# An FFT convolution block: times split 64 by 16 with two groups of times on the partitions, smaller tiles in the first and last step, a new order

## The chip, the cores and the metric

The kernel runs on one core of one Trainium2 chip. The metric is the device time in microseconds (us). Five engines work side by side, each through its own queue in order: PE (matmuls, with PEld loading weights), DVE, ACT, POOL (named G in the order below) and SP, which here only issues transfers. Transfers run on 16 DMA engines.

## The reference

```python
def _A_ref(q, k, v, shift_k, ssm_k, ssm_D):            # 2048 times, 512 channels
    k_shift = sum(k_pad[:, t:t + S, :] * shift_k[:, ks - 1 - t] for t in range(4))
    kv = k_shift * v
    y = irfft(rfft(kv, padded to 2S) * rfft(ssm_k, padded to 2S))[:, :S]   # long convolution
    y = y + kv * ssm_D
    return q * y
...
x = A_q
h = x + _A_ref(_layernorm(x), A_k, A_v, A_shift_k, A_ssm_k, A_ssm_D)
h2 = h + _B_ref(_layernorm(h), B_w1, B_w2, B_w3, B_w4)
```

`_B_ref` is a block with four matmuls: layer norm, w1 (512 x 512), GELU, a shift in time by -1, +1, -2 and +2 of four groups of channels, w2, a residual, then layer norm, w3 (512 x 1792), GELU, w4 and a residual. All inputs and the output are bfloat16.

## The kernel before

The 2048 times are cut into two halves s of 1024. Time t = 1024 s + 8 p + b lies on partition p, in block b (0 to 7); so a row of `q`, `v` and the output is 8 consecutive times of one half. The long convolution is done by halves, with odd-frequency transforms of length 2048 of each half of the filter (F0, F1) and of kv (A0, A1). The first half of y is A0 x F0, the second A0 x F1 + A1 x F0. The transform of 1024 times is split 32 by 32, p = 4 n + l.

The steps, with the short names that are used here; a name is followed by its half or signal and numbers (S1:F0.3.0):

- Lf, Lk, Lv, Lq: loads of the filter, of k (already transposed, with the taps of the short filter behind each row), of v and q. K (L432) is the short convolution as matmuls against diagonals of the taps (dg, L295); KV (L446) multiplies it by v on DVE.
- S1 (step1, L382): first step, 128-row matmuls onto 32 columns; the table f1 is zero where a row belongs to another l. E1 copies PSUM to bfloat16. X (L405): eight transfers of 256 KB per signal, SBUF to SBUF, that exchange partition and block. S2 (step2, L408): second step, on 64x32 tiles. E2 copies out, or for F1 combines with F0.
- P (L474): products of spectra on DVE; I2 (L484): first inverse step, on 32x64 tiles; EV copies out; XI (L495): 16 transfers of 256 KB in all that bring the result back into the order of times; I1 (inv1, L498): last inverse step, full 128x128 matmuls, two accumulated.
- H (L615): q (y + ...) by DVE, with Y the normalised q (its row statistics are Q, L505, then QV, QP, QN). HS, uw, rr, hn: layer norms. hb, lb: normalised rows; LT/TE and LX/EX transpose them, by PE (flip) or by DMA (turn). W, U: w1 and GELU; X2: w2; S, R: sums; M, G: w3 and GELU; O: w4; Z: the last sum; OUT: store.

What runs in which order is written out by hand as a string, ORDER: each word has the number of a task, its engine (P, V for DVE, A, G for POOL, S for SP) and its PSUM slots. Tasks are added with their dependencies in `body`; a program emits them in ORDER's order, so each engine's queue stands in the order of its words, and an instruction that waits holds all that stands behind it on its engine. The figures in braces in the `add` calls are a planner's costs and set nothing at run time. The buffer r_z holds the first-step results of A1 and also receives XI, so S1 of A1 waits for I1 of the first half (the zdeps of forward1, L395).

SP's queue begins with the loads of the first half; Q:0.0 to Q:0.7 stand on DVE behind the KV of the first half.

Of the kernel before, what the change touches and what calls it, by code (L numbers as in the profile page):

```python
# [17 lines left out]
KW = NB * 129 + 8  # L18
# [13 lines left out]
004S 029P0 000S 002S 003S 005S 008S 031V 037V 001S 030P 063P23 006S 055P45 009S 057P67 064V 007S 056A 038G 065P01 010S 058A 019S 059P45 033V 045G  # L32
061P23 060A 087P60 039G 036V 062A 095P71 046V 042V 066A 093P4 032G 043V 047A 074S 101P5 044A 034G 015S 094V 051P23 022S 088V 053P01 035G 023S 052A
040V 072S 089P4 024S 054A 049G 091P6 021S 090V 073S 041A 097P2 096V 050G 070S 092V 099P3 048A 069S 102V 068S 107P01 098V 109P67 017S 100V 108A 103P45
067S 110V 111P23 018S 104A 115P01 071S 113P67 112A 323V 105P45 324V 116A 211P20 106V 114A 117P01 212V 119S 118A 084P4567 326V 085A 081P2301 123S 329V
086V 120S 083A 215P4 020S 082A 330V 124S 078P0167 327V 125S 217P5 080A 216V 121S 079A 075P2367 012S 218V 011S 325V 076A 127P4501 016S 319V 328V 122S
077A 219P21 129V 126S 331G 128A 013S 220V 130P6701 139V01 132A 141V23 131A 133P4501 332G 134A 140P23670 147V45 142P 135A 333G 149V67 143A 337G0
148P45011 155V01 150P 343G1 144A 145S 221P2 340G2 157V23 152A 146S 334G3 014S 151A 136P6701 222V 137V 138A 156P23452 153S 158P 154S 163V45 225P0 159A
223P1 160A 165V67 161S 164P67230 162S 226V 166P 224V 175P45 167A 168V 213P0 176A 169S 183P67 214V 170S 185P23 184A 187P45 315S 186V 177P01 188A 189P67
178V 179P23 190A 181P45 180V 171P67 028S 182A 172P01 338V 192S 231P45 196S 335V 339A 349G0 173P23 316S 344V 336A 346G3 193S 341V 235P67 232A 355G1  # L40
195S 347V 174P10 236A 352G2 191S 350V 237P45 198S 358G 342A 356V 202P6723 197S 348A 353V 194S 345A 359G 204V 239P01 238A 371G 203V 241P23 240A 227P45
242A 229P01 372G 360V 228V 230A 199P6723 247S 361G0 373V 233P45 351A 364G1 200V 362P00 234A 374G2 365P1 384V 366A 377G3 208P6745 245S 363V 354A 375P11
243S 201V 385G 367P0 376A 244S 357A 378P1 386V 246S 369P2 379A 390V0 318S 209V 397G 387A1 382P3 248S 370A 250S 388P12 210V 368A 398G 391P6 249S 380P7
383A 389A 027S 392V 399G 251P2345 263V01 381A 393P0 253A 026S 400G3 265V23 395P1 025S 252A 317S 403V2 205P6745 396A 267V45 401P23 394A 404P3 502P1
402A 206V 405A 506P0 503V 408P2 507V 504A 406P3 269V67 508A 409A 264P67011 558V 407A 266P 207V 268P 559G 270P 560G 498P2 271A 272V 561G1 510P3 564G0
499V 274S 494P4 501V 273S 562P50 511V 565P6 514P7 563A 495V 566A 411V 254P0123 496A 567P50 515V 256A 275V01 569P4 568A 577P6 277V23 570A 257P2345 578A
412V 573P7 259A 255V 571P6 258A 279V45 579P4 572A 574A 281V67 575P5 580A 516A 276P01232 414V 500A 278P 513V 280P 576A 615G 512V 282P 581P6 505V 283A
616G 517V 284A 617G 413V 621G3 287V01 618A2 619P71 587G 622P4 582V 260P0123 620V 583S 584P5 623V 588G 262A 289V23 589G 291V45 591A1 590G0 293V67
624P40 593S 261V 636P6 592S 625A 634P7 416V 509V 288P23010 635A 594S2 290P 299V01 292P 285S 294P 301V23 628P4 296A 632P7 303V45 629A 298S 637A 626P0
286S 633A 305V67 630P1 295A 410V 627A 297S 300P67231 417V 631A 302P 415V 304P 306P 418V 641P4 307A 419G 308A 309S 310S 420V 421V0 427G3 638P0 424G1  # L50
430V2 585V 642V 497V 311P16 639V 312P72 640S 422V 643S 313P35 425V 423A 433G0 428V 314P40 426A 431V 439A3 595P10 445G 442V1 432A 603P2 436V2 429A 437V
597P6 596A 434V 446G 605P7 598A 438A 447V 599P1 448V2 435A 451G3 322V 458V 607P5 600A 470V 459G 449P33 452P6 601P1 450V 453A 471G 460V 604A 440V 454P6
602A 472G 441V 461A2 456P3 443V 474G1 462A3 444V 473G0 608A 476S 606A 612P2 482V 475S 457A 463S 483G 464S 609P1 484V 477S0 485A1 486G0 455A 487S 321V
488S 465S1 518P0 522P3 489S2 480P4 523V 478P5 519V 524A 468P3 520A 481A 466P7 644V 521V 645G 490P6 467A 525V 646G 469A 492P0 610V 320G 479A 647V2
534P3 491A 648V3 649S 493A 650S 542P4 535V 554P5 537V 536A 538P3 651S3 555V 546P7 543V 556A 586S 545V 526P1 544A 611S 539V 530P6 547V 540A 550P3 527V
672G 652P00 529V 531V 658P1 673G 528V 656P5 659A 674V 532V 653A 675G1 662P4 657A 549V 676G0 660P7 551V 678S 654P5 552V 661A 677S 664P3 553V 655A 756G
548A 533V 663A 679S0 700V 665A 666P6 701G 702V 703V3 704G2 613V 669P7 757G 667V 706S 705S 541V 758G 557V 759G0 728G 680P10 729G 686P0 681A 730V 731V1
682P5 732G2 670V 687A 688P4 684P3 707S1 760G3 689A 692P2 668S 761S 693A 733S 685A 734S 708P60 714P4 735S2 712P1 720P0 671S 713A 762S 710P2 721A 715A
716P3 711A 736P10 683A 763S3 717A 742P0 709A 614S 737A 748P6 743A 738P4 749A 764P50 772P7 776P6 774P2 777A 765A 766P3 775A 768P6 767A 773A 744P5 769A
740P1 770P0 741A 739A 771A 778P2 718P4 779V 780S 719A 725P3 722P4 726V 727S 781P7 723V 724S 690P4 782V 783S 691A 697P6 745A 694P7 746P1 695V 698V 696S  # L60
747A 750P0 699S 753P2 751V 752S 754V 755S
# [32 lines left out]
def body(ctx, tc, fx, kt, q, v, sd, w1, w2, w3, w4, out):  # L94
# [18 lines left out]
    HX = 130  # L113
# [8 lines left out]
    r_h = raw("r_h", DC * NB * HX)  # L122
# [7 lines left out]
    kT = [[kw[:, s, c, 0:NB * 129].rearrange("p (b x) -> p b x", b=NB) for c in range(DC)] for s in range(2)]  # L130
    kvs = r_kv[:].rearrange("p (g b d) -> p g b d", g=2, b=4)

    def z1v(r):
        return view(r, 0, G, "p (b h d) -> p b h d", b=4, h=4)
# [10 lines left out]
    wv = view(r_z, 0, G, "p (k h d) -> p k h d", k=NB, h=2)  # L145
# [3 lines left out]
    h1T = [view(r, 0, DC * NB * HX, "p (c b x) -> p c b x", c=DC, b=NB) for r in (r_h, r_f0)]  # L149
# [6 lines left out]
    GHOME = ((r_v, NB * D), (r_kv, 0), (r_v, NB * D), (r_kv, 0), (r_f0, DC * NB * HX), (r_a0, 0), (r_a0, GS), (r_f1, 0))  # L156
    gbs = [view(r, lo, GS, "p (f x) -> p f x", f=FC) for r, lo in GHOME]
    nbx = ct("nbx", 2, D)
    nbt = [r_k[:, DC * F:DC * F + D], r_k[:, DC * F + D:DC * F + 2 * D], nbx[:, 0, :], nbx[:, 1, :]]
# [8 lines left out]
    f1 = ct("f1", 8, 2, 2, 2, 4)  # L168
    f2 = ct("f2", 2, 32, 4)
# [41 lines left out]
    u1a, u1b = early(64), [early(64)]  # L211
    pool.iota(u1a.rearrange("p (t h c k) -> p t h c k", t=2, h=4, c=2), pattern=[[2048, 2], [128, 4], [0, 2], [512, 4]], base=32, channel_multiplier=0)
    pool.iota(u1b[0].rearrange("p (a c k) -> p a c k", a=8, c=2), pattern=[[0, 8], [1024, 2], [0, 4]], base=3072, channel_multiplier=0)
    l4 = small("l4", 4)
    pool.iota(l4[:], pattern=[[1, 4]], base=0, channel_multiplier=0)
    pn = small("pn", 2)
    vec.tensor_scalar(out=pn[:, 0:1], in0=pi[:], scalar1=2, scalar2=None, op0=SHR)
    vec.tensor_scalar(out=pn[:, 1:2], in0=pi[:], scalar1=3, scalar2=None, op0=AND)
    nf = small("nf", 2, F32)
    vec.tensor_copy(nf[:], pn[:])  # L220
    s1 = early(64, BF16)
    mk = small("mk", 4, F32)

    vec.scalar_tensor_tensor(out=u1b[0], in0=u1a, scalar=nf[:, 0:1], in1=u1b[0], op0=MUL, op1=ADD)
    vec.tensor_scalar(out=u1b[0], in0=u1b[0], scalar1=4095, scalar2=None, op0=AND)
    act.activation(s1, u1b[0], ACT.Sin, bias=negpi[:], scale=SC)
    vec.tensor_scalar(out=mk[:], in0=l4[:], scalar1=nf[:, 1:2], scalar2=None, op0=OP.is_equal)
    for i in range(2):
        for j in range(2):
            vec.tensor_scalar(out=f1[:, :, i, :, j, :], in0=s1.rearrange("p (a c k) -> p a c k", a=8, c=2),  # L230
                              scalar1=mk[:, 2 * i + j:2 * i + j + 1], scalar2=None, op0=MUL)
    make_identity(nc, ident[:])
    wf = early(72, F32).rearrange("p (o b) -> p o b", o=9)
    pool.memset(wf[:, 0:8, :], 0.0)
    for o, terms in enumerate((((4, 16), (2, 8), (0, 4), (1, 2), (5, 1)), ((6, 64), (7, 1)), ((3, -1024), (7, 3072)), ((3, 3072),),
                               ((5, 4), (6, 8), (0, 128), (1, 256), (2, 512), (3, 1024), (4, 2048)), ((6, 64), (0, 16), (1, 32), (2, 8), (7, 1)),
                               ((3, -3072), (7, 3072)), ((5, 2), (4, 1)))):
        for b, w in terms:
            pool.memset(wf[:, o, b:b + 1], float(w))
# [192 lines left out]
    def shift(g, c):  # L432
        s, b4 = divmod(g, 2)

        def f(e, sl):
            o = ps[:, sl[0], :]
            for i, d in enumerate((0, 1, 2, 3, -1, -2, -3)):
                j0, j1 = max(0, -d), min(3, 3 - d)
                bb, x = 4 * b4 + d, 1
                if bb < 0:  # L440
                    bb, x = bb + NB, 0
# [402 lines left out]
```

## Time and profile before

| what | value |
|---|---|
| runs | 214.49, 215.71, 216.97 us; median 215.71 |
| the profiled execution | 213.26 us, of which the span is 211.6 |
| granted TensorE clock | 1.000 |
| PE / DVE / ACT busy, 0 to 60 us | 51.3 / 55.5 / 50.4 us |
| PE / DVE / ACT busy, 60 to 114 us | 51.8 / 50.1 / 35.9 us |
| PE / DVE / ACT busy, 114 to 212 us | 92.6 / 39.2 / 39.3 us |
| DMA share and rate in these three stages | 0.84 and 286 GB/s; 0.58 and 174; 0.27 and 64 |
| first products (P) begin | 30.4 us |
| I1 of the first half begins, of the second half | 48.5 us, 113.9 us |

The page gives busy times per engine over the span and in 40 equal slices (a digit is tenths of a slice), the chain of waits followed back from the last instruction, and the costliest groups of instructions. A group's line has the line of the kernel, the engine, the operation, its output and input tiles with sizes, the count, the busy time and the mean duration. The answers by stage list, for each stretch, the busy time of each engine with the number of instructions in brackets, then the granted clock, the mean share of the 16 DMA engines and the rate. Transfers are listed with their size and the time from issue to landing:

```profile
r_z<-r_vs SPq DMA_DIRECT2D x16, 256.0 KB, 3.9
r_k<-in_kt_dram SPq DMA_DIRECT2D x8, 260.0 KB, 4.6
r_v<-in_v_dram SPq DMA_DIRECT2D x4, 512.0 KB, 7.3
r_f<-r_f SPq DMA_DIRECT2D x8, 256.0 KB, 5.2
r_q<-in_q_dram SPq DMA_DIRECT2D x8, 256.0 KB, 5.7
...
out_dram<-r_v SPq DMA_DIRECT2D x16, 128.0 KB, 1.9
```

r_z<-r_vs is XI; r_f<-r_f is X of F0; out_dram is OUT.

### The profile page before, as it was taken

The numbers are of one execution on the slowest core, as the hardware profiler recorded it, in microseconds if no ns is written. First come the engines' busy times: TensorE is split into PE (matmuls) and PEld (weight loads), VectorE is DVE, ScalarE is ACT, GpSimd is POOL, SyncE is SP. The second block draws the span as 40 slices with busy tenths as digits, with TensorE's granted clock in tenths as the row PEclk, the third lists the DMA queues.
The fourth block names the chain that finished last, engine by engine and source line by source line (L and its number), as shares of the span: only waits on it lengthen the run. The fifth ranks groups of instructions, "written<-read, shape, count | busy, mean of one in ns | idle before, by whom it ended". The sixth has DMA issues, their size and how long they took to land.

```text
span 211.6 us, 5040 instructions
## 1 busy us (share of the span) xinstructions
PE 195.7 (93%) x1964; PEld 116.2 (55%) x1980; DVE 144.8 (68%) x302; ACT 125.5 (59%) x206; POOL 80.1 (38%) x177
## 2 busy tenths in 40 slices
PE   6899769898889999979999999989999999999992
PEld 5454323442248546636744884645848888645450
DVE  6998999999999999999868971559972000112031
ACT  3979989787999658943751883364623565301010
POOL 7850059804888140287044683212765000000000
PEclk9999999999999999999999999999999999999999
DMA  6999895976948995000693008533146440010011
GB/s 173 313 403 397 321 325 222 256 205 237 371 169 294 332 435 147 0 28 13 89 232 92 27 22 181 98 69 82 42 107 154 102 74 0 3 50 34 16 50 50
DMA packets 30809, 32.86 MB, mean 155 GB/s; under 512 B 20545, under 2 KB 22594, under 8 KB 30530
## 3 DMA queue, kind: packets, MB, share of 16 engines
q1 hardware_dynamic: 30786, 32.55, 50.8%
q8 instruction: 15, 0.25, 0.5%
q14 instruction: 8, 0.07, 0.1%
HBM read 13.14 MB, written 4.46 MB: 83 GB/s over the span
## 4 chain that ended last, share of the span: by engine, by line
PE 59%; DVE 13%; ACT 12%; DMA 6%; issue 3%; POOL 3%; SPq 3%; DVEq 0%; ACTq 0%; POOLq 0%
PE ps L777 21%; PE ps L790 18%; ACT r_a L257 5%; PE ps L722 5%; PE ps L699 5%; PE ps L484 3%; DVE r_v L616 3%; DMA r_dg<-dhb 2%; DMA r_a<-r_a 2%; PE ps L502 2%; PE ps L413 2%; DMA r_k<-in_kt_dram 2%; DVE r_f L425 2%; DVE r_dg L307 1%; DVE r_p L474 1%
## 5 line engine op out<-in xcount | busy, mean ns | idle before, releaser
L777 PEld LDWEIGHTS <-r_k 128*128 128x128 bf16 x448 | 43.5, 98 | 7.7 <-issue 1.2
L792 DVE TENSOR_TENSOR r_v<-ps,r_v 128x512 bf16<-128x512 f32 x16 | 10.7, 686 | 42.4 <-PE ps L790 42.4
L474 DVE TENSOR_TENSOR r_p<-r_a,r_f 128x2048 bf16<-128x2048 bf16 x24 | 28.7, 1240 | 1.0 <-PE ps L484 0.6
L777 PE MATMUL ps<-r_dg,r_k 128*128 128x256 bf16 x224 | 25.6, 273 | 0.1
L257 ACT CAST r_a<-ps 128x1024 bf16<-128x1024 f32 x23 | 22.2, 1026 | 3.0 <-PE ps L413 2.8
L781 ACT ACTIVATE r_f<-ps 128x512 bf16<-128x512 f32 x14 | 7.8, 599 | 20.6 <-PE ps L777 20.6
L613 POOL TENSOR_SCALAR z_t<-r_q,qrs,qnm 128x512 f32<-128x512 bf16 x11 | 13.0, 1188 | 12.6 <-DVE r_v L616 12.0
L442 PE MATMUL ps<-r_dg,r_k 128*128 128x256 bf16 (+3 forms) x108 | 15.2, 284 | 1.6 <-ACT r_f L257 0.8
L257 ACT CAST r_vs<-ps 128x1024 bf16<-128x1024 f32 x14 | 13.7, 1032 | 4.9 <-PE ps L484 4.9
L725 DVE SCALAR_TENSOR_TENSOR r_q<-r_v,hrr,ps 128x512 bf16<-128x512 bf16 x16 | 11.4, 742 | 5.9 <-PE ps L722 3.7
L781 ACT ACTIVATE r_a<-ps 128x512 bf16<-128x512 f32 x14 | 7.8, 606 | 12.2 <-PE ps L777 12.2
L257 ACT CAST r_f<-ps 128x1024 bf16<-128x1024 f32 x14 | 13.2, 1023 | 3.0 <-PE ps L389 2.8
L442 PEld LDWEIGHTS <-r_k 128*128 128x128 bf16 x112 | 9.5, 98 | 9.5 <-issue 4.8
L484 PE MATMUL ps<-r_p,ttab 32*64 32x512 bf16 x384 | 13.3, 379 | 1.0 <-DVE r_p L474 0.8
L699 PEld LDWEIGHTS <-r_fx 128*128 128x128 bf16 x128 | 12.3, 98 | 3.2 <-DMA r_dg<-dhb 0.6
L600 ACT ACTIVATE junk<-r_v 128x512 bf16<-128x512 bf16 x14 | 8.9, 635 | 7.3 <-DVE r_v L616 7.1
L777 PE MATMUL ps<-xtx,r_k 128*128 128x256 bf16 x112 | 13.0, 273 | 0.0
L600 ACT ACTIVATE junk<-r_q 128x512 bf16<-128x512 bf16 x12 | 7.6, 630 | 9.2 <-DVE r_q L725 9.1
L777 PE MATMUL ps<-xty,r_k 128*128 128x256 bf16 x112 | 12.7, 272 | 0.0
L790 PE MATMUL ps<-w4s,r_f 128*128 128x512 bf16 x54 | 12.5, 379 | 0.1
L748 POOL TENSOR_TENSOR xrr<-xrr,mhalf 128x2 f32<-128x2 f32 x8 | 7.2, 900 | 14.2 <-DVE xrr L745 13.8
L389 PEld LDWEIGHTS <-f 128*32 128x32 bf16 x256 | 6.1, 95 | 11.3 <-issue 7.5
(183 smaller groups left out, 374.7 us busy)
## 6 DMA issues: line engine op xcount, KB each, us to landing
r_z<-r_vs SPq DMA_DIRECT2D x16, 256.0 KB, 3.9
r_k<-in_kt_dram SPq DMA_DIRECT2D x8, 260.0 KB, 4.6
r_v<-in_v_dram SPq DMA_DIRECT2D x4, 512.0 KB, 7.3
r_f<-r_f SPq DMA_DIRECT2D x8, 256.0 KB, 5.2
r_q<-in_q_dram SPq DMA_DIRECT2D x8, 256.0 KB, 5.7
r_a<-r_a SPq DMA_DIRECT2D x8, 256.0 KB, 4.2
r_f<-r_a SPq DMA_DIRECT2D x8, 256.0 KB, 4.2
r_a<-r_z SPq DMA_DIRECT2D x8, 256.0 KB, 4.1
```

The lines of the kernel that those rows point to most:

```text
L257: (act.copy if e in "AM" else on[e].tensor_copy)(o, i)
L442: nc.tensor.matmul(o[:, (d + j0) * P:(d + j1 + 1) * P], lhsT=kT[s][c][:, bb, x:x + P], rhs=diag[:, c, j0:j1 + 1, :].rearrange("p j x -> p ...
L474: on[e].tensor_tensor(out=prs[:, sl[0]:sl[0] + 2, :, :], in0=sp[a][:, kl, :, :, :], in1=gv, op=MUL)
L484: nc.tensor.matmul(ps[64 * t:64 * t + 64, bk[h], :], lhsT=ttab[32 * h:32 * h + 32, 2 * kl + t, 2 if x else xx, :], rhs=prs[32 * h:32 * h + ...
L600: act.activation(junk[:], x, ACT.Square, accum_out=sq[:, i, 1:2])
L613: on[e].tensor_scalar(out=z_t[:, sl[0], :], in0=qs, scalar1=qrs[:, i:i + 1], scalar2=qnm[:, i:i + 1], op0=MUL, op1=ADD)
L699: nc.tensor.matmul(ps[:, sl[0], j * 256:(j + 1) * 256], lhsT=w1s[:, k, m * P:(m + 1) * P], rhs=xt[:, k, :], start=(k == 0), stop=(k == DC ...
L725: vec.scalar_tensor_tensor(out=q_sb[:, s, b, :], in0=h_sb[s][:, b, :], scalar=hrr[:, 4 * s + b // 2, 0, b % 2:b % 2 + 1], in1=ps[:, got((" ...
L777: nc.tensor.matmul(ps[:, sl[0], j * 256:(j + 1) * 256], lhsT=w3s[:, k, fc * P:(fc + 1) * P], rhs=xt[:, k, :], start=(k == 0), stop=(k == D ...
L781: act.activation(gb[:, 2 * fp:2 * fp + 2, :], ps[:, got(("M", s, p, fp))[0], :].rearrange("p (j x) -> p j x", j=2), ACT.Gelu_apprx_tanh)
L790: nc.tensor.matmul(ps[:, sl[0], :], lhsT=gb[:, fc, (b % 2) * P:(b % 2 + 1) * P], rhs=w4s[:, fc, :], start=(fc == 0), stop=(fc == FC - 1))
L792: add(("Z", s, b), {V: 0.61}, lambda e, sl, b=b: vec.tensor_tensor(out=h_sb[s][:, b, :], in0=ps[:, got(("O", s, b))[0], :], in1=h_sb[s][:, ...
```

## The change

A time is now t = 1024 s + 16 n + 8 q + b, on partition 64 q + n: the transform is split 64 (n) by 16 (q and b), and the two groups q lie on the two partition halves. The first step contracts 64 rows of one group (64x32 tiles, no zeros in f1), the last step writes 64 columns of one group (128x64 tiles). Loads and stores of q, v and the output, the packing of k, and the layout of the shifted activations h1T follow the new order of times; h1T and k keep some blocks twice, so that a shift by a block can cross from one group into the other (copies du). In the diff below the two `dma_start` pairs are X and XI. X reads every eighth partition (16) and writes all 128; XI is 32 transfers of 128 KB and writes every sixteenth partition (8). The taps' diagonals are built on POOL alone, four row statistics of the second half go to ACT, the sine tables are smaller, and ORDER is a new one. The counts of matmuls stay as they are.

```diff
     def z1v(r):
-        return view(r, 0, G, "p (b h d) -> p b h d", b=4, h=4)
+        return view(r, 0, G, "p (l q g h d) -> p l q g h d", l=2, q=2, g=2, h=2)
...
-    wv = view(r_z, 0, G, "p (k h d) -> p k h d", k=NB, h=2)
+    wv = z1v(r_z)
...
-    v_r = v.rearrange("o (s p b) d -> p (o s) b d", s=2, b=NB)
-    q_r = q.rearrange("o (s p b) d -> p (o s) b d", s=2, b=NB)
-    o_r = out.rearrange("o (s p b) d -> p (o s) b d", s=2, b=NB)
+    v_r = v.rearrange("o (s n q b) d -> q n (o s) b d", s=2, q=2, b=NB)
+    q_r = q.rearrange("o (s n q b) d -> q n (o s) b d", s=2, q=2, b=NB)
+    o_r = out.rearrange("o (s n q b) d -> q n (o s) b d", s=2, q=2, b=NB)
...
-        add(("dg", c), {V: 0.8, A: 1.19, GP: 0.85}, dg(c), [("Lk", 0, c)], port="VG")
+        add(("dg", c), {GP: 0.65}, dg(c), [("Lk", 0, c)], port="VG")
...
-    def step1(b, hp, *srcs):
+    def step1(b, hh, src):
...
-                            nc.tensor.matmul(ps[32 * j:32 * j + 32, sl[hh], :], lhsT=tab[:, 4 * t + 2 * hp + hh, :], rhs=src(2 * b + b0),
+                    for qq in range(2):
+                        nc.tensor.matmul(ps[32 * j:32 * j + 32, sl[qq], :], lhsT=f1[64 * qq:64 * qq + 64, 2 * t + hh, :], rhs=src(2 * b + b0)[64 * qq:64 * qq + 64],
+                                         start=True, stop=True)
...
-                    nc.sync.dma_start(z2[sig][g:P:2, kl, :, :], z1[sig][kl:P:4, 2 * g:2 * g + 2, :, :])
+                        nc.sync.dma_start(z2[sig][:, x // 2, 2 * (x % 2):2 * (x % 2) + 2, :], z1[sig][x:P:8])
...
-            for hp in range(2):
-                    wv[4 * hp + kl:P:8], vst[:, got(n, "vs")[0], 2 * hp:2 * hp + 2, :]), [("EV", s, kl, hp)] + wd, size=256, drop=[(n, 0, "vs")])
+            for h in range(4):
+                    wv[4 * kl + h:P:16], vst[:, got(n, "vs")[0], h, :]), [("EV", s, kl, h // 2)] + wd, size=128, drop=[(n, 0, "vs")])
...
     def inv1(s, b):
...
-                for h in range(2):
-                    nc.tensor.matmul(ps[:, sl[b0], :], lhsT=f2[:, h].rearrange("p n q -> p (n q)"), rhs=wv[:, 2 * b + b0, h, :], start=(h == 0), stop=(h == 1))
+                for qq in range(2):
+                    nc.tensor.matmul(ps[64 * qq:64 * qq + 64, sl[b0], :], lhsT=f2[:], rhs=wv[:, b % 2, qq, b // 2, b0, :], start=True, stop=True)
...
     def qstat(s, b):
+        if s == 0 or b < 4:
+            return lambda e, sl: vec.bn_stats(qst[:, 8 * s + b, :], q_sb[:, s, b, :])
...
+            act.activation(junk[:], q_sb[:, s, b, :], ACT.Identity, accum_out=qst[:, 8 * s + b, 0:1])
+            act.activation(junk[:], q_sb[:, s, b, :], ACT.Square, accum_out=qst[:, 8 * s + b, 1:2])
...
+        add(("du", s, 0), {GP: 0.4, V: 0.2}, lambda e, sl, s=s: on[e].tensor_copy(hend[s][0][:, :, :, 1:64], hend[s][0][:, :, :, 128:191]), [("U", s, 3, 0)], port="VG")
+        add(("du", s, 1), {GP: 0.4, V: 0.2}, lambda e, sl, s=s: on[e].tensor_copy(hend[s][1][:, :, :, 128:191], hend[s][1][:, :, :, 1:64]), [("U", s, 0, 1)], port="VG")
...
-KW = NB * 129 + 8
+KW = 5 * P + 3 * 192 + 8
```

SP's new order begins, by name: Lf:0.2, Lk:0.3, the row of D, Lf:0.0, Lk:0.0, Lk:0.2, Lk:0.1, Lq:0.1, Lv:0.0, Lv:0.1, Lf:0.3, Lq:0.3, Lk:1.0, Lf:0.1, Lv:1.0, Lq:0.2, Lk:1.3, Lq:0.0, then six X of F0, Lk:1.2, four X of A0, two X of F0, three X of A0, Lv:1.1, the last X of A0, Lf:1.1, Lf:1.0, Lf:1.3, Lk:1.1, Lf:1.2, and the sixteen XI of the first half. On DVE Q:0.3 and Q:0.2 stand ahead of the first KV, and Q:0.0 after KV:2.0, ahead of Q:0.4, Q:0.5, KV:2.3 and the evictions of the second step. Later Lw1, Lw2, five X of F1, Lq:1.3 and three X of F1 follow, and Lq:1.2, Lq:1.1 and Lq:1.0 stand between the XI of the second half; Q:1.1, Q:1.0, Q:1.3 and Q:1.2 stand on DVE ahead of the products of kl 2 and 3, Q:1.5 on ACT ahead of the first GELUs (G:0.1).

## The prediction

> **What bounds the kernel now.** I read the page first (shares, and the slices of the span), then the chain of waits, then DMA share and rate by stage, then single rows. From the page:
>
> ```profile
> span 211.6 us, 5040 instructions
> PE 195.7 (93%) x1964; PEld 116.2 (55%) x1980; DVE 144.8 (68%) x302; ACT 125.5 (59%) x206; POOL 80.1 (38%) x177
> PE   6899769898889999979999999989999999999992
> DVE  6998999999999999999868971559972000112031
> DMA  6999895976948995000693008533146440010011
> ```
>
> 93% of PE is an average. A slice is 5.3 us: up to slice 11 (60 us) DVE is as full as PE, and the DMA engines are full too; from slice 20 on only PE is. The chain of waits names the same stages (start, length, what):
>
> ```profile
> 2.49 4.02 DMA r_k<-in_kt_dram
> ...
> 25.47 4.66 DMA r_a<-r_a
> ...
> 39.54 2.90 DVE r_p L474 x2
> ...
> 48.50 0.38 PE ps L502
> ...
> 113.92 3.61 PE ps L502 x16
> ```
>
> Loads, the reordering transfers X, DVE's products and the last step I1 carry the first 60 us; then matmuls follow each other. DMA by stage (the last two numbers are the share of the 16 engines and the rate):
>
> ```profile
> 12.00:16.00 4.00, 3.87 (x41) 2.36 (x31) 4.00 (x8) 3.92 (x5) 2.91 (x5) 1.00 1.04 400
> 38.00:44.00 6.00, 5.30 (x92) 2.57 (x90) 5.83 (x7) 4.05 (x5) 3.37 (x4) 1.00 0.97 255
> 56.00:58.00 2.00, 1.45 (x24) 0.43 (x19) 1.85 (x7) 2.00 (x3) 1.60 (x6) 1.00 1.03 418
> 107.00:111.00 4.00, 3.84 (x47) 1.74 (x32) 2.14 (x12) 1.93 (x2) 2.11 (x2) 1.00 1.08 234
> ```
>
> Loads and X (rows 1 and 3) run at 400 to 418 GB/s. XI (rows 2 and 4) keeps the engines just as busy and moves 234 to 255. XI is the transfer whose list on one side begins with only 16 rows; X has 32 and 64, the loads 128. So how a list begins sets the rate. And the steps that the change is about (start, length, count):
>
> ```profile
> 43.06 0.61 PE L389 MATMUL ps<-r_q,f 128*32 128x512 bf16 x8
> 43.60 1.05 PE L442 MATMUL ps<-r_dg,r_k 128*128 128x512 bf16 x7
> ...
> 66.55 0.62 PE L413 MATMUL ps<-r_a,ftab 64*32 64x512 bf16 x16
> 67.11 0.61 PE L699 MATMUL ps<-xtx,r_fx 128*128 128x256 bf16 x4
> ```
>
> Starts count, since ends are modelled: eight of the old first step take 0.54 us (43.06 to 43.60), sixteen matmuls on 64x32 tiles 0.56 (66.55 to 67.11).
>
> **The change, part by part.** *First step.* 32 groups of eight go from 0.54 to half of 0.56: 32 x 0.26 = 8.3 us of PE. All stand before 60 us, where PE is busy 51.3 us, DVE 55.5 and ACT 50.4; I cost it at nothing there, since DVE's and ACT's queues cover it.
>
> *Last step.* Sixteen matmuls of 3.61 us become 32 in pairs of column tiles, a shape that the trace lacks. Between no overlap (7.2) and full overlap (1.8) I take 1.8, because the column tiles of the first step nearly overlap (0.54 for eight is 0.068 each, a full matmul takes 0.226). The first half's I1 lies in DVE's stage, the second half's in PE's: -1.8.
>
> *DVE, ACT, POOL.* The eight tap diagonals on DVE (3.1 us at 6.5) become two more on POOL (0.64 each); the tables shrink. The four row statistics that go to ACT (0.61 on DVE; there two activations and reads, 2 x 0.82) lie in DVE's full stage, and ACT has room. By counting each queue with the rows' durations, DVE from the first product to the last falls from 72.1 to 69.1 us. The new copies (du, four of 0.3 to 0.6 by the edge copies' rows) and the kt rows, 18% longer (0.79 instead of 0.66 us each), are small. All that: -2 at most.
>
> *X and XI.* The eight X per signal keep their size, but read 16 rows instead of 32, and wait for all eight evictions instead of four. Their issue costs 0.57 each as before. XI becomes 32 of 128 KB instead of 16 of 256: 16 x 0.56 = 9 us more of SP, of which the last four issues cost 1.1 us on the way to I1. On the destination an XI list now begins with 8 rows. By halving the rows of the 107 to 111 us window it would run at half of 234, 117 GB/s: 1.1 us each; if rows did not matter, 0.33.
>
> *Lq, Lv and OUT.* This decides. Times are now split 64 by 16 with the two groups q on the partition halves, so the DRAM side of v_r, q_r and o_r begins with a step of **2** (q), then 64 rows, where it was 128. No transfer of the trace begins so. Bounds: unchanged, 0.66 us per 256 KB (400 GB/s); or shared out by the outer step, two engines. One engine moves 400 / 1.04 / 16 = 24 GB/s. I calculate with 24.7 (395 GB/s at share 1.02 from 10 to 20 us): 5.3 us for an Lq, 10.6 for an Lv, 2.65 for an OUT. The nearest row is XI, the shortest beginning, and it is slowed nearly in proportion; so I take two engines.
>
> [...]
>
> Now the sum on the two engines, in SP's order, starting at 2.1 us (an estimate: the first matmul that needs a load starts at 3.6, less 0.66 and a tail of 0.8). Every other transfer has a sixteenth on them (0.66 per 256 KB, Lk 0.79). Two Lf and four Lk: 6.6. Lq 11.9. Two Lv 33.1. Lf, Lq, Lk, Lf: 40.5. Lv 51.1, Lq 56.4, Lk 57.2, Lq 62.5. Eight X of F0, seven of A0, Lk: 73.2. Lv (second half) 83.8. The last X, four Lf, Lk: 87.9. Who waits: on DVE the statistics Q:0.3 and Q:0.2 stand ahead of the gating KV, so DVE's whole queue waits for Lq at 11.9, then KV for the Lv at 22.5 and 33.1, and Q:0.0 stops it until 62.5; behind it stand evictions of F0 and A0, hence S2 on PE, hence the products, which begin at about 71 (30.4 now). The sixteen XI have, dealt to 8 engines, 0.66 each on these two: twelve end at 95.8, the last four at 98.5; a landing tail of 1.6 (an OUT lands in 1.9, of which 0.33 moves data) gives I1 at 100.1, against 48.5 now: **+51.6**.
>
> After I1 the rest follows as before, plus: Lq:1.3 (5.3) stands before three X of F1, S2 waits about 2; the other three Lq (16 us) start only behind XI of the second convolution, and Q:1.1 on DVE and Q:1.5 on ACT stand in front of products and GELUs: I estimate 4; the last OUT 2.65 instead of 0.33: 2.3; I1: -1.8. Sum 51.6 + 2 + 4 + 2.3 - 1.8 = **+58**. On the profiled execution (213.26 us: span 211.6 and 1.7 around it) this is 271; the median of the runs shown is 215.71 (214.49 to 216.97), 2.45 above that execution. I say 272.
>
> **The rivals.** *Loads at full rate, narrow SBUF lists slow.* For: the XI windows above. Against: X has never read 16 rows here. XI at 117 GB/s takes 16 x 1.1 = 18 us for the first convolution; from its first eviction at 34.6 it ends at 52.6, and I1 starts at 54 instead of 48.5: +6. If X's reads fall to 234 GB/s too, the sixteen X of F0 and A0 take 18 us instead of 11: another 4 to 8, since S2 waits for them. With 1 for the second convolution and -2 for the rest: +5 to +13, 221 to 229, 225 in the middle. [...]
>
> *No transfer is slowed (the other side).* Then DVE's stage starts its products about 0.5 us sooner (ACT's evictions in front of them bind: 18 instead of 21 of 0.93 us, but one idle spell more), PE's part after 60 us loses 1.8 with I1, and the 1.1 us that PE waited for two layer-norm rows at 92.6 and 93.7 go, as the new order puts that transposition two stages later. Against it about 1.4: after I1 PE now reaches the first DMA-transposed tile after 16 us of work, where 17.5 are needed (evictions, two writes of 2.1 us, a transposition of 3.1 landing). That is 215.7 - 2 = 213.7. It decides if an Lq lands within 6 us under load as now (5.7 on the page) while the others run.
>
> *The matmul tiles do not overlap*: then the first step is no dearer than now (0.54), the last costs +3.6 on PE; this changes no sign and only matters in the previous case: 219.
>
> **How the numbers follow.** Two engines: 0.62. Narrow lists alone: 0.20. No slowing: 0.18, of it 0.10 faster by over 1%, 0.05 within 1% (2.2 us, about what a measurement here can tell, with runs spread over 2.5), 0.03 slower. Slower in all 0.85. The likeliest case's own range is 258 (engines 10% faster, which takes 9 off the sum, and the estimates of 4 and 2 at nothing) to 284 (XI 1.1 instead of 0.66 on those engines, 7 to 10 more, and more OUT in the way of late transpositions). With the second case the range is 219 to 284; outside are the third case and little more.
>
> **What would show it.** Right: Lq and Lv landing 5 us and more after they begin to move, a DMA share near 0.13 and 50 GB/s for long stretches before 60 us; DVE idle with in_q and in_v as releasers; I1 near 100 us, and from there to the end about 98 us as now plus 6. The first step's eight at 0.28 and sixteen of I1's old work in 1.8 show the PE terms. Wrong: 350 GB/s and more through the loads; then the forecast falls by 45 us at once, and XI's share against its rate between the products and I1 tells the second case from the third.

## The result and the profile after

| | before | after |
|---|---|---|
| median of the runs | 215.1 us (214.17 to 216.97) | 319.24 us (315.82 to 321.14) |
| the profiled execution's span | 211.6 us | 317.4 us |
| first products (P) begin | 30.43 us | 77.67 us |
| I1 of the first half begins | 48.5 us | 120.25 us |
| from there to I1 of the second half | 65.4 us | 87.4 us |
| from there to the end | 97.7 us | 109.8 us |

The ratio is 1.477 (95% interval 1.460 to 1.495). The forecast was 272 us, in a range from 219 to 284. Ratios, and the times of the experiments below, leave out disturbed executions, those over 1.5% longer than the kernel's fastest; loads_128 and v_only keep one execution each, so they have no interval, and their stretches come from a disturbed one and are a few us too long. From the page of the changed kernel, the rows that were shown of before, with the granted clock (in tenths) and the rate:

```profile
span 317.4 us, 5061 instructions
PE 207.7 (65%) x1963; PEld 118.2 (37%) x1980; DVE 145.7 (46%) x299; ACT 131.9 (42%) x218; POOL 84.2 (27%) x187
PE   5900452047518506599959989089999986999960
DVE  6501442028715706769852896076579620000420
PEclk9975558558958756679995999879999999899995
DMA  6121312959815596279721045512620534300111
GB/s 219 57 80 53 110 52 84 238 134 214 227 63 109 117 214 169 73 183 318 270 74 50 18 75 103 95 35 67 134 66 3 112 74 86 75 2 4 43 48 39
```

A slice is 7.9 us here. Apart from one slice of PE, none of the five engines is full any more in the first eight. From the second slice to the seventh the DMA engines are at one to three tenths and at 52 to 110 GB/s, where before they were full, at up to 400. By stage (PE, PEld, DVE, ACT, POOL busy, the granted clock, the share of 16 engines, the rate):

```profile
15.00:19.00 4.00, 1.00 (x9) 0.51 (x7) 0.36 (x1) 1.04 (x2) 1.20 (x3) 1.00 0.13 53
24.00:30.00 6.00, 0.00 (x0) 0.00 (x0) 1.29 (x2) 0.00 (x0) 0.00 (x0) 0.50 0.13 53
68.00:74.00 6.00, 5.31 (x56) 1.83 (x55) 2.64 (x4) 3.64 (x4) 0.00 (x0) 0.50 0.96 225
100.00:108.00 8.00, 4.83 (x69) 2.23 (x70) 4.12 (x5) 3.15 (x4) 0.00 (x0) 0.80 0.57 105
196.00:206.00 10.00, 2.85 (x14) 1.08 (x11) 2.73 (x5) 0.00 (x0) 0.90 (x2) 0.89 0.56 99
```

Three kinds of transfer, three signatures. The loads Lq and Lv (rows 1 and 2): 0.13 of 16 is 2.1 engines, 53 GB/s together, 25 each; in the trace's records of single packets 2.0 are under way at a time from 24 to 30 us. X (row 3): all engines, but 225 GB/s, 14 each. XI (rows 4 and 5): 0.56 of 16 is nine engines (a full set reads up to 1.08 on this scale, so eight), and 99 to 105 GB/s, 12 to 13 each. So a few engines at full rate, or all of them at half rate, or half of them at half rate. Who waits for the loads, on DVE (start, length, what; in brackets the idle time before it and what ended it):

```profile
14.07 1.29 DVE L494 BATCH_NORM_STATS2 qst<-r_q 128x6 f32<-128x512 bf16 x2 [3.21 <-DMA r_q<-in_q_dram]
24.43 1.29 DVE L437 TENSOR_TENSOR r_kv<-ps,r_v 128x512 bf16<-128x512 f32 x2 [9.07 <-DMA r_v<-in_v_dram]
35.48 2.48 DVE L437 TENSOR_TENSOR r_kv<-ps,r_v 128x512 bf16<-128x512 f32 x4 [9.76 <-DMA r_v<-in_v_dram]
...
66.37 1.88 DVE L494 BATCH_NORM_STATS2 qst<-r_q 128x6 f32<-128x512 bf16 x3 [12.88 <-DMA r_q<-in_q_dram]
```

These are the waits that the forecast put at 11.9, 22.5, 33.1 and 62.5. What it missed comes later. The queue of SP in the stretch from 80 us, and at the end:

```profile
83.99 25.26 SPq L482 DMA_DIRECT2D r_z<-r_vs  x16
```

```profile
273.50 34.75 SPq L795 DMA_DIRECT2D out_dram<-r_v  x9
```

Sixteen XI keep SP for 25 us, and what follows them on the queue starts only then. And from the chain of waits:

```profile
198.17 9.01 DMA r_z<-r_vs
207.18 0.46 issue
207.64 3.33 PE ps L489 x16
...
306.31 0.69 DVE r_v L793
```

I1 of the second half waits 9 us for XI, and the last Z ends at 307.0, 10.4 us before the span does; in the kernel before, these were 3.1 us (208.5 and 211.6). In these 10 us two engines drain OUTs (share 0.13, 48 GB/s from 306 to 316 us).

### The profile page after: what moved, and what is told of

It reads as the page before. It is cut to its first block, busy times and chain, and to the rows that moved or that the text cites. A ratio compares the mean times of both kernels' runs of the same rounds, so it can differ in the third digit from the quotient of the medians.

```text
span 317.4 us, 5061 instructions
## 1 busy us (share of the span) xinstructions
PE 207.7 (65%) x1963; PEld 118.2 (37%) x1980; DVE 145.7 (46%) x299; ACT 131.9 (42%) x218; POOL 84.2 (27%) x187
## 5 line engine op out<-in xcount | busy, mean ns | idle before, releaser
L437 DVE TENSOR_TENSOR r_kv<-ps,r_v 128x512 bf16<-128x512 f32 x16 | 10.6, 688 | 36.8 <-DMA r_v<-in_v_dram 30.6
L615 POOL TENSOR_SCALAR z_t<-r_q,qrs,qnm 128x512 f32<-128x512 bf16 x11 | 12.9, 1179 | 48.3 <-DVE r_v L618 47.7
L401 PE MATMUL ps<-r_f,ftab 64*32 64x512 bf16 x128 | 7.7, 500 | 21.9 <-DMA r_f<-r_f 18.1
L429 PE MATMUL ps<-r_dg,r_k 128*128 128x256 bf16 (+3 forms) x107 | 20.5, 350 | 1.9 <-issue 1.2
L364 PE MATMUL ps<-r_fx,f 64*32 64x512 bf16 x64 | 4.4, 613 | 25.6 <-DMA r_fx<-in_fx_dram 23.1
L618 DVE SCALAR_TENSOR_TENSOR r_v<-ps,qsd,z_t 128x512 bf16<-128x512 f32 x16 | 11.4, 746 | 20.8 <-PE ps L489 19.0
L489 PE MATMUL ps<-r_z,f 128*64 128x512 bf16 x32 | 7.1, 582 | 19.8 <-DMA r_f<-r_a 11.0
L401 PEld LDWEIGHTS <-ftab 64*32 64x32 bf16 x256 | 3.5, 94 | 44.3 <-issue 20.6
L364 PEld LDWEIGHTS <-f 64*32 64x32 bf16 x256 | 4.1, 101 | 41.0 <-DMA r_fx<-in_fx_dram 22.9
L507 POOL TENSOR_TENSOR qnm<-qst 128x8 f32<-128x8 f32 (+1 forms) x2 | 0.8, 422 | 69.4 <-DVE qst L494 69.4
L494 DVE BATCH_NORM_STATS2 qst<-r_q 128x6 f32<-128x512 bf16 x12 | 7.9, 684 | 23.8 <-DMA r_q<-in_q_dram 23.8
L401 PE MATMUL ps<-r_a,ftab 64*32 64x512 bf16 x128 | 7.4, 430 | 14.9 <-DMA r_a<-r_a 10.7
```

The lines of the kernel that those rows point to most:

```text
L401: nc.tensor.matmul(ps[32 * h:32 * h + 32, sl[2 * t + r], :], lhsT=ftab[64 * t:64 * t + 64, 4 * kl + h, r, :], rhs=z2[sig][64 * t:64 * t + ...
L429: nc.tensor.matmul(o[:, (d + j0) * P:(d + j1 + 1) * P], lhsT=kw[:, s, c, x:x + P], rhs=diag[:, c, j0:j1 + 1, :].rearrange("p j x -> p (j x ...
L437: vec.tensor_tensor(out=kvs[:, got(("K", g, 0), "kv")[0], :, c * P:(c + 1) * P], in0=ps[:, got(("K", g, c))[0], :].rearrange("p (b x) -> p ...
L489: nc.tensor.matmul(ps[64 * qq:64 * qq + 64, sl[b0], :], lhsT=f2[:], rhs=wv[:, b % 2, qq, b // 2, b0, :], start=True, stop=True)
L615: on[e].tensor_scalar(out=z_t[:, sl[0], :], in0=qs, scalar1=qrs[:, i:i + 1], scalar2=qnm[:, i:i + 1], op0=MUL, op1=ADD)
L618: vec.scalar_tensor_tensor(out=h_sb[s][:, b, :], in0=ps[:, got(("I1", s, b // 2))[b % 2], :], scalar=qsd[:, i:i + 1], in1=z_t[:, got(("Y", ...
```

## The experiments

Theory: all three signatures cost time, and they add up. Lists that begin with 2 get two engines (share 0.13), XI's lists that begin with 8 get eight (0.56); and apart from that, the places of X's and XI's rows in SBUF halve the rate of each engine (12 to 14 GB/s instead of 25). Rivals: the two engines are all of it; the rows are all of it; the new order costs time of its own.

The changed kernel was repaired piece by piece. In the table every row from loads_128 to all_wide_16 contains the repairs above it, v_only is a part of loads_128. Of the last five rows, before_2 and before_x32 change the kernel before, out_only the changed kernel, and two_starts_xi and x_two_queues start from xi_rows. The times are medians, the last three columns stretches of the profiled execution.

| kernel | time, us | ratio to before (95%) | to I1, first half | to I1, second half | to the end |
|---|---|---|---|---|---|
| before | 215.1 | | 48.5 | 65.4 | 97.7 |
| after | 319.1 | 1.477 (1.460 to 1.495) | 120.3 | 87.4 | 109.8 |
| v_only | 281.8 | | 86.3 | 88.0 | 110.1 |
| loads_128 | 258.4 | | 72.9 | 82.6 | 109.6 |
| loads_out | 248.3 | 1.156 (1.146 to 1.165) | 69.9 | 78.1 | 96.9 |
| xi_rows | 228.8 | 1.066 (1.059 to 1.073) | 61.1 | 72.1 | 96.1 |
| x_wide | 216.4 | 1.009 (1.003 to 1.015) | 53.4 | 65.8 | 95.5 |
| all_wide | 214.8 | 1.003 (1.000 to 1.007) | 50.9 | 65.7 | 96.1 |
| all_wide_16 | 214.4 | 1.001 (0.997 to 1.005) | 51.1 | 64.7 | 96.6 |
| before_2 | 283.8 | 1.321 (1.316 to 1.325) | 104.6 | 80.1 | 97.7 |
| out_only | 302.7 | 1.415 (1.404 to 1.427) | 119.3 | 84.5 | 98.1 |
| two_starts_xi | 230.4 | 1.076 (1.069 to 1.084) | 62.3 | 69.4 | 95.8 |
| before_x32 | 220.8 | 1.029 (1.024 to 1.035) | 53.7 | 65.9 | 97.9 |
| x_two_queues | 231.0 | 1.073 (1.065 to 1.081) | 65.8 | 67.3 | 96.2 |

**Loads alone: loads_128 and v_only.** The inputs are laid out in the order of the partitions, so that one list step covers 128 rows.

```diff
-    v_r = v.rearrange("o (s n q b) d -> q n (o s) b d", s=2, q=2, b=NB)
+    v_r = v.rearrange("o (s p b) d -> p (o s) b d", s=2, b=NB)
...
+    lay = lambda x: x.reshape(2, 64, 2, NB, D).transpose(0, 2, 1, 3, 4).reshape(1, S, D)
```

(q in the same way; v_only has it for v alone.) Of loads_128 was expected:

> The changed kernel with q and v laid out in DRAM in the order of the partitions, so that the lists of Lq and Lv begin with 128 rows again; X, XI, OUT and the order of all queues stay as changed. Theory (both happen: loads and OUT on two engines, and X and XI slowed by their few rows): the load stage is repaired, XI still moves 95 GB/s (1.35 us each, 21.6 for sixteen), so I1 of the first half begins at 62 to 66 us instead of 120, OUT still drains 8 us late: 243 us (235 to 250). Rival 1 (two engines are all of it, XI only looks slow because the loads stand in its queue): XI falls to 0.66 us each and I1 to about 52: 225. Rival 2 (few rows in X and XI are the main cost, the loads merely wait with them): over 290.

258.4 us, from one execution. Rival 2 is out: the loads alone bring back about 61 of the 104 us. Rival 1 is out too: at 258 much is left. The theory's own 235 to 250 was missed as well: I1 came at 73 (70 in loads_out), not at 62 to 66, which had priced XI as slow but X as before; x_wide below puts X's rows at 7.7 us up to I1. Of v_only was expected:

> The changed kernel with the list of v alone begun with 128 rows; Lq and OUT stay on lists that begin with 2. Theory (one queue, so on the two engines every byte ahead counts, whoever it is for): four Lv give back 4 x (10.1 - 1.3) = 35 us and the Lq keep 4 x (5.0 - 0.7) = 17: I1 of the first half begins at about 85 instead of 120, 284 us. Rival (the row statistics on DVE, which wait for Lq and stand ahead of the gating, are what holds everything): v alone gives less than 20, over 300 us.

281.8 us and I1 at 86: v gives 37.3 us, q the other 23.4, again from one execution each. The plain sum over the queue had 35 for the four Lv and 17 for the four Lq ahead of I1; q has four more Lq behind I1. So the statistics on DVE are not what holds the kernel.

**The list alone, in the other kernel: before_2.** The kernel before, its q and v laid out so that two steps of 64 rows bring the same bytes to the same places.

```diff
-    v_r = v.rearrange("o (s p b) d -> p (o s) b d", s=2, b=NB)
+    v_r = v.rearrange("o (s n g b) d -> g n (o s) b d", s=2, g=2, b=NB)
```

> The kernel before, with q and v laid out in DRAM so that the lists of Lq and Lv begin with 2 steps of 64 rows; nothing else is touched and the same bytes land in the same places. Theory (two engines): an Lq takes 5.0 us and an Lv 10.1 on them; by the sum over the queue I1 of the first half begins at about 92 instead of 48.5, and the time is 255 to 265 us. Rival 2 (the DRAM list does not matter, only the rows in SBUF): unchanged, 215 us.

283.8 us: the first number of a DRAM list costs this kernel 69 us, with nothing else touched but the order of the rows in DRAM. By the stretches, 56 of them lie ahead of the first I1 and 15 between the two. That is more than the 255 to 265 of the theory. Its transfers in 12 to 16 us, a window that before had at share 1.04 and 400 GB/s:

```profile
12.00:16.00 4.00, 1.16 (x19) 0.34 (x16) 0.43 (x1) 2.53 (x3) 0.00 (x0) 1.00 0.13 52
```

I1 began at 104.6, though, not at 92. The reason stands in DVE's queue:

```profile
84.86 0.69 DVE L450 TENSOR_TENSOR r_kv<-ps,r_v 128x512 bf16<-128x512 f32 x1 [8.11 <-DMA r_v<-in_v_dram]
85.47 2.35 DVE L474 TENSOR_TENSOR r_p<-r_a,r_f 128x2048 bf16<-128x2048 bf16 x2
```

The KV that waits for the fourth Lv stands ahead of the products, so these begin at 85.5; from there to I1 are 19.1 us of work, as the 18.1 of before. I had put XI right behind the last load in the queue and left this work out.

**OUT: loads_out and out_only.** Each OUT as two transfers of 64 rows, once with the loads repaired, once alone.

```diff
-nc.sync.dma_start(o_r[:, :, s, b, :], h_sb[s][:, b, :])
+[nc.sync.dma_start(o_r[i, :, s, b, :], h_sb[s][64 * i:64 * i + 64, b, :]) for i in range(2)]
```

> As the last one, and each OUT as two transfers of 64 rows, so that its list no longer begins with 2. Theory: the tail between the last Z and the end falls from about 10 us to about 3, and the XI of the second half no longer stand behind OUTs: 8 to 9 us less than the last one, 234. Rival (the OUT tail is a tail of late work, not of the two engines): within 3 us of the last one.

> The changed kernel with OUT alone in two transfers of 64 rows; the loads stay on two engines. Theory (OUTs queue on the two engines, eight of 2.65 us in the last 35 us, whatever went before): 10 to 13 us less than the changed kernel, 307. Rival (with everything late the OUTs drain beside other work): within 3 us, 316 or more.

About 10 us less after the loads were repaired (where loads_128 has one execution), 16.4 less alone; both more than expected, while the 234 of loads_out was missed with the base it was counted from. In both the last stretch falls to what it was before (96.9 and 98.1). So the OUT tail does not depend on what went before.

**XI's rows: xi_rows.** The eight rows of an XI stand 4 apart instead of 16. The rows of f2 are permuted with them by other weights for the bits of the partition number, so the kernel computes the same.

```diff
-                    wv[4 * kl + h:P:16], vst[:, got(n, "vs")[0], h, :])
+                    wv[32 * kl + h:32 * kl + 32:4], vst[:, got(n, "vs")[0], h, :])
```

> As the last one, and XI writes 8 rows that stand 4 apart instead of 16 apart (the rows of f2 are permuted with it, so that the same thing is computed). The list still begins with 8 rows, so it still has half of the engines. [...] Rival (eight engines, or the short runs of 1 KB, set XI's rate): XI stays at 95 to 100 GB/s and the time within 2 us of the last one.

228.8 us, 19.5 less by the medians, where I had put 12 to 16, on the estimate that XI's eight engines come from 12 to 13 GB/s each back to about twice that (15.7 between the two profiled executions, of which one is its kernel's shortest run and the other its longest). XI by stage, first in loads_out, then in xi_rows:

```profile
47.00:50.00 3.00, 2.93 (x54) 1.52 (x52) 3.00 (x4) 2.46 (x3) 0.00 (x0) 1.00 0.58 107
```

```profile
48.00:53.00 5.00, 4.85 (x84) 2.24 (x83) 5.00 (x7) 4.28 (x5) 0.00 (x0) 1.00 0.56 195
```

The same share, the same eight engines, the same number of rows and bytes, and nearly twice the rate. So it is the place of the rows, not their number and not the runs of 1 KB. Eight engines at the loads' 25 GB/s would give 200 (an estimate), and xi_rows comes to 195.

**X's rows: x_wide and before_x32.** In x_wide X reads half of 32 rows 4 apart instead of all of 16 rows 8 apart; in before_x32, the kernel before, 32 adjoining rows instead of 32 rows 4 apart. Both exchange other rows than the transform needs, with sizes and counts as they were.

```diff
-z1[sig][x:P:8])
+z1[sig][x % 4:P:4, x // 4])
```

```diff
-z1[sig][kl:P:4, 2 * g:2 * g + 2, :, :])
+z1[sig][32 * kl:32 * kl + 32, 2 * g:2 * g + 2, :, :])
```

> As xi_rows, but each X reads half of 32 rows that stand 4 apart instead of all of 16 rows that stand 8 apart (256 KB and runs of 2 KB as before; another exchange than the transform needs). [...] Rival (what is left between xi_rows and the kernel before comes from the new order and from more issues, not from X): 227 to 229.

> The kernel before, with X reading 32 adjoining rows instead of every fourth row (another exchange than the transform needs; sizes, lists, counts and order are as before). [...] Rival (what counts is how many rows a list has): unchanged, 215.

216.4 us (12.3 less, more than the 6 to 9 that I had put with X near 400 GB/s, an estimate from its 418 in the kernel before) and 220.8 us (6.6 more than the kernel before beside it, at 214.3; I had put 222 to 226 us with X at 220 GB/s, an estimate from its 225 in the changed kernel). The second has the same number of rows and differs only in where they stand, so the rival that counts rows is out. X with other traffic, in xi_rows, in x_wide and in before_x32:

```profile
28.00:36.00 8.00, 4.17 (x60) 1.36 (x55) 4.40 (x6) 4.14 (x5) 5.95 (x15) 0.79 0.95 224
```

```profile
26.00:32.00 6.00, 3.90 (x57) 1.18 (x58) 4.95 (x6) 4.72 (x6) 4.41 (x13) 0.91 0.94 333
```

```profile
24.00:28.00 4.00, 2.42 (x30) 1.27 (x31) 3.78 (x6) 3.64 (x5) 0.00 (x0) 1.00 1.03 265
```

In before_x32 all engines are busy as before (share 1.03) and the rate is 265 GB/s, not 220.

**What is then left: all_wide and all_wide_16.** XI writes half of 16 rows 8 apart (another order than the last step needs), first in 32 transfers, then in 16.

```diff
-wv[32 * kl + h:32 * kl + 32:4], vst[:, got(n, "vs")[0], h, :])
+wv[2 * kl + h // 2:P:8, h % 2], vst[:, got(n, "vs")[0], h, :])
```

> As the last one, and XI writes half of 16 rows that stand 8 apart (still 32 transfers of 128 KB, runs of 1 KB; another order than the last step needs). [...]

> As the last one, with XI again as 16 transfers of 256 KB: now every list is as in the kernel before, except that OUT goes in two. Theory (all that the change loses is transfers): the time comes to the case in which no transfer is slowed, 213 to 216 us. Rival (the new order, or the wait of X for all eight evictions, costs several us of its own): 218 or more.

214.8 and 214.4 us: 16 rows at the head of XI's list instead of 8 give 1.6 us by the medians (I had put 1 to 3), with intervals that overlap, and half of the issues give nothing that is clear of the noise. XI in all_wide_16:

```profile
40.00:45.00 5.00, 4.84 (x91) 2.45 (x77) 4.50 (x6) 4.03 (x6) 0.34 (x1) 1.00 1.06 212
```

Twice the engines of xi_rows (share 1.06 instead of 0.56) move hardly more, 212 instead of 195 GB/s, here in transfers of 256 KB. So, as far as these rows show, the two limits do not multiply: the lower one sets the rate, the engines in xi_rows (195 against an estimate of 200) and the place of the rows here.

With lists as in the kernel before (X writes 128 rows instead of 64, OUT goes in two) the changed kernel takes as long as the kernel before (ratio 0.997 to 1.005), so the new order, the smaller tiles and the longer wait of X lose nothing together and win nothing that could be measured. In this kernel the steps on PE can be read at full clock (start, length, count):

```profile
51.65 0.62 PE L364 MATMUL ps<-r_kv,f 64*32 64x512 bf16 x16
52.21 1.04 PE L489 MATMUL ps<-r_z,f 128*64 128x512 bf16 x4
```

```profile
115.83 1.92 PE L489 MATMUL ps<-r_z,f 128*64 128x512 bf16 x16
```

Sixteen of the first step in 0.56 us by their starts, sixteen of the last step in 1.9.

**Two ways to repair it: two_starts_xi and x_two_queues.** The first leaves q and v as given and issues every Lq and Lv as two transfers of 64 rows. The second is xi_rows with half of the X, those of the source rows 4 to 7 of each 8, on ACT's queue.

```diff
+        add(name, {SP: 0.9}, lambda e, s: [nc.sync.dma_start(dst[64 * i:64 * i + 64], src[i]) for i in range(2)], deps)
```

```diff
-                        nc.sync.dma_start(z2[sig][:, x // 2,
+                        (nc.scalar if x > 3 else nc.sync).dma_start(z2[sig][:, x // 2,
```

> As xi_rows (XI on rows 4 apart, OUT in two transfers), but with q and v in DRAM as given and each Lq and Lv issued as two transfers of 64 rows onto one half of the partitions: the repair without another layout of the inputs. [...]

> [...] Rival (X is held by the engines' rate from SBUF to SBUF in runs of 2 KB): 229 or more.

two_starts_xi takes 230.4 us. Its loads do run at 250 GB/s from 10 to 18 us, at share 1.05, but against xi_rows this costs about 2 us, where I had put 6. A reason could be that the X behind them, at 224 GB/s, were the longer queue anyway; no run shows that. x_two_queues takes 231.0 us, no gain, where I had put 220 to 225. In it the transfers together reach 293 GB/s at share 1.03 from 23 to 27 us, where xi_rows had 224 in its stretch of X; a few loads are mixed into both, so it is not shown that the two sets of rows together move more than one of them. The products still begin at 39.5 instead of 35.7 us, probably because ACT issues and waits ahead of its copies; that was not tried by itself. No version that computes the reference was faster than the kernel before.

## Why the prediction was wrong

Right: the direction, and the mechanism that carried most of it up to the first I1. Loads on two engines were put at 5.3 us for an Lq and 10.6 for an Lv; at the measured 53 GB/s they are 4.9 and 9.9. The sum on the two engines fits the waits of DVE within 4 us as far as 66 us. By the repairs, Lv and Lq are about 61 of the 104 us. The way to it was partly luck: XI before, at 234 to 255 GB/s, was taken for the nearest row, "slowed nearly in proportion" to how its list begins. But its share was 0.97 to 1.08, all engines, and the runs show no loss from the beginning of its list: in all_wide_16, where XI goes onto the same kind of rows at 212 GB/s, the time is as before, while the place of the rows alone doubles a rate in xi_rows. So this row said nothing of two engines.

The profiled execution is 47.7 us longer than the sum had it: 20.2 of them lie ahead of the first I1, 27.5 behind it, where XI and X were again taken at the speed of before and all OUT but the last at nothing (the first point below).

Ahead of I1, wrong was above all the price of XI. "If rows did not matter" XI was 0.33 us, and of the two engines' share I put 0.66; the 1.1 of halved rows stood only in the upper bound, and narrow rows as a whole stood among the rivals, as if they excluded the two engines. They come on top: 128 KB at 99 GB/s is 1.32 us. The records of single packets in the trace show it. Apart from a first hundred of their 2048 packets, the sixteen XI run from 94.4 to 118.8 us, 24.4 us where 10.6 were put. Sixteen times 0.66 more are 10.6 of the 13.8; the rest lies in their last eighth, which takes 8 us (110.7 to 118.8). The loads of w1 and w2 and X of F1, issued right behind, move beside it (a share of 1.06 from 112 to 118 us); the sum had left them out, and that they are the cause was not tried. I1 begins 1.45 after the last packet, for which 1.6 was put. That an XI is dealt to eight engines at 0.66 us each is a term of the sum that no run had shown; the runs showed a share of 0.56, which fits eight, and 1.32 us each.

The other 6.6 us are there before XI begin (94.4 instead of 87.9): 3.9 already when Q:0.0 has its data at 66.4, the rest behind that, with X among it. X moves 225 GB/s, so 256 KB take 1.17 us instead of 0.66, and sixteen would add 8.2; no more than about 2.7 of that reached I1 here.

Point by point:

- *The time after the first I1.* Put at +2, +4, +2.3 and -1.8, 6.5 together; measured 22.0 in the middle stretch and 12.1 in the last, 34. In the middle, by the repairs, XI's rows are 6.0 us, X's rows 6.3, OUT about 4.5 (the ones between the XI; 2.9 by out_only) and the loads about 4.8, for which 6 was put. In the last stretch it is OUT (109.8 falls to 98.1 in out_only). Each was sized rightly (2.65 us; 128 KB at 48 GB/s is 2.7), but only the last one was counted, and the ones before it still stood on the same two engines. OUT on the whole costs 10 to 16 us, not 2.3.
- *First step, last step.* 0.28 us for eight and 1.8 for the last step; measured 0.28 and 1.9. The count was wrong: the last step has sixteen matmuls for each half, as before, not 32 (the page has x32 for both). So no overlap would have been 3.6 us, as before, not 7.2, and the rival's +3.6 would have been nothing. That the first step gains nothing before 60 us fits all_wide_16, whose I1 is not earlier than before.
- *DVE, ACT, POOL: -2 at most.* Not seen. In all_wide_16, which leaves the rest of the change bare, I1 comes 2.6 us later than before and the two later stretches are 1.8 shorter.
- *The rival in which no transfer is slowed*, 213.7: all_wide_16 takes 214.4, in a spread (212.6 to 215.2) that holds it.
- *The rival of narrow rows alone*, +5 to +13 and 225 in the middle: loads and OUT repaired, the kernel takes 248.3, so +33. Up to the first I1 the sizes were near: X 4 to 8, measured 7.7 (x_wide); XI 6, measured 8.8 for the place of its rows (xi_rows) and 2.6 for 16 of them instead of 8 at the head of its list (all_wide). The second half was put at 1 and took 12.3 in the middle stretch (6.0 for XI, 6.3 for X): there I1 waits 6.7 us in loads_out and 0.6 in xi_rows. Which wait carries the 6.3 of X is not shown.

So the step that failed is that the two cases were kept apart: the range took in each case alone and not both together, although the rows of XI in the profile of before, 234 to 255 GB/s at a share of 0.97 to 1.08, had already shown a rate far below the 400 of the loads where engines are not lacking. The shares of 0.13 and 0.56 fit 2 engines for Lq, Lv and OUT and 8 for XI; the place of the rows told at the same time: XI moves 99 to 105 GB/s on this share here and 195 in xi_rows.

## What to carry to other kernels

Read two things off every transfer before a layout is changed: what the outer step of each list is, on the DRAM side too, and where its rows stand in SBUF. The share of the engines against the rate told them apart here: a share of 0.13 at the usual 25 GB/s per engine went with lists that begin with 2, a share of 0.96 at 14 per engine with X's rows 8 apart, and XI had both, 0.56 at 12 to 13. As far as XI shows, the lower of the two limits then sets the rate: it moved 99 to 107 GB/s on eight engines with rows 16 apart, 195 on eight with rows 4 apart, 212 on sixteen with rows 8 apart. Where such a transfer shares a queue, price every one of them that stands ahead, not only the one that somebody waits for.

## What the runs showed of the hardware that was not expected

The granted clock of TensorE was 1.000 throughout the profiled execution before; in the changed kernel it is 0.826 on the mean and falls to 0.50 where PE stands idle (24 to 30 us, no PE work at all), and it is still 0.50 from 68 to 74 us, where PE is busy for 5.3 of 6 us. Sixteen matmuls of I1 take 3.33 us behind 9 us of idle time, against 1.92 in all_wide_16. In these stretches the clock is low behind idle time. No run made it a cause by itself, so what it adds to the 104 us is not known; all_wide_16 is as fast as before at a mean of 0.968.

Permuting the rows of one small table was enough to nearly double the rate (107 to 195 GB/s at shares of 0.58 and 0.56) of a transfer that keeps its size, its list and its engines (xi_rows): what the transform needs leaves open where its rows stand.
